# Attention and a gated product on one core: three loads issued by ScalarE, the second weights laid four rows to a partition, and four written orders shifted

## The chip, the cores and the metric

The kernel runs on one core of one Trainium2 chip. The core has five engines that run their own instruction streams: TensorE (PE, with its weight loads shown apart as PEld), VectorE (DVE), ScalarE (ACT), GpSimd (POOL) and SyncE (SP), which here only issues DMAs. The metric is the device time of one execution in microseconds, from the first instruction to the last transfer.

## The reference

Eight batches of eight heads, 576 positions, 64 values a head. Every position attends to those at most 32 away; then every token (a row of 512 = 8 heads x 64) goes through two products with a gelu between.

```python
scores = q @ k.T / sqrt(64)                  # per batch and head, 576 x 576
scores = where(|i - j| <= 32, scores, -1e9)
attn   = softmax(scores);  x = attn @ v      # then 4608 tokens x 512
h      = x @ w_in                            # 512 -> 2048
g      = 0.5 * h * (1 + tanh(sqrt(2/pi) * (h + 0.044715 * h**3)))
out    = g @ w_out                           # 2048 -> 512, fp32
```

All inputs and the output are fp32 in the chip's memory; on the chip the kernel computes in fp16 with fp32 sums.

## The kernel before, in words

**Tiles of tokens.** The 4608 tokens are nine tiles of 512 (t = 0 to 8), which straddle the batches of 576. A stage of the loop over t (line 893) does the first product of tile t, 16 blocks of 128 hidden units ("columns") by four 128-row parts of w_in (`ffn_in`, line 526), each followed by a gelu on ACT (`gelu`), and then the second product. Into the steps of that second product the attention of batch t + 1 is woven. Attention of batch 0 stands ahead of the loop.

**Weights.** w_in (512 x 2048) and w_out (2048 x 512) are read once, in quarters of 1 MB, as fp32 into buffers of a ring of five (`stage`), and cast to fp16 into w_in16 and w_out16, which stay. The SBUF layout of w_out16 is 16 row blocks of 512 columns; row block fc must hold the rows that belong to the hidden units of column block fc of w_in16. Before, both are in natural order: partition p of row block fc is row 128 fc + p (`w_out_v`, line 227), and the casts of w_in (`cast_w`, line 240; lines 835 to 849 and 875) copy 512 columns straight. w_in's casts are shared by POOL, ACT and DVE, w_out's by POOL, ACT and DVE inside tile 0's second product.

**Loads.** Nearly all loads are issued by SP in the order of the program: queries and keys of batch 0 in pairs of heads (`qk`), the keys' tail (positions 512 to 575, `tails_0`), the values' tail (`vs(4)`, line 256), the values of each head (`v_of_pair`), the quarters of w_in, and then w_out's quarters mixed with the queries, keys and values of batch 1 (lines 822 to 861). The query tail of batch 0 (line 852) and the values' tail of batch 1 (in `vs(2, 3, 4)`, line 859) stand among them. "wo3b" below is the second half of the last quarter of w_out (line 860), which holds row blocks 14 and 15.

**Orders written out by hand.** No planner places the work: the program's order is each engine's order. Four tables set it around the change.

- ORDER_0 (line 70) is the order of tile 0's second product, 64 matmuls of 512 columns: steps 0 to 47 take row blocks 0 to 11, each for four token blocks, steps 48 to 55 blocks 12 and 13, steps 56 to 63 blocks 14 and 15.
- PLAN_0 (line 53) names what is put ahead of which step: "s" scores of a group of two heads (4 groups, and -1, the tail), "m" its mask on DVE, "r" the transposes of a pair and their copies, "k" the casts for them, "w" and "u" casts of w_out, "e" casts and "d" copies of the values, "n" the sums of two groups with their logarithms on ACT, "p" the products with the values, "v" both for one group, "x" the division into xT, "c" differences of w_out for later.
- PLAN_1 (line 66) is the same for tile 1 with its 112 matmuls of 256 columns; PLAN serves the later ones.
- MIX (line 62) is the first product of tiles 7 and 8, of which half the columns go by seven block products for two units, A and B, with sums instead of eight (Winograd's form): a number is a plain column, "A3" a block product, "s" a copy of a bank, "c" a sum with one, "g" a gelu, "t" and "u" the sums that the second product needs. In `in_mixed` (line 600) the copies "s" are on ACT for n = 1 and on DVE else.

The second product of tiles 1 to 8 (`ffn_out`, line 700) is also in Winograd's form: seven products of 16 matmuls, whose results DVE reads and adds (lines 730 to 757).

Of the kernel before, what the change touches and what calls it, by code (L numbers as in the profile page):

```python
# [9 lines left out]
FP32 = mybir.dt.float32  # L10
# [26 lines left out]
def cut(b):  # L37
# [12 lines left out]

PLAN_0 = {4: "s0@0", 9: "r1@1", 14: "s1@0", 15: "w1", 16: "m0", 19: "k2", 22: "r2@1", 23: "m1", 25: "s2@0", 27: "t-1@1",
# [3 lines left out]

MIX = ("3 g3 A0 s0A B0 s0B A2 B2 cA00 cB00 A1 s1A A4 B1 s1B gA00 gB00 B4 t0 u0 12 A3 s3A B3 s3B g12 cA11 cB11 13 "
       "A5 B5 gA11 gB11 g13 14 gA10 gB10 A6 B6 cA01 cB01 g14 15 gA01 gB01 t1 t2 g15 t3 u1 u2 u3").split()
UNITS = {"A": 1, "B": 2}

PLAN_1 = {12: "s0@0 s1@1 s2", 16: "m0 m1", 36: "m2", 56: "s-1@0 v0@1 v1", 64: "m-1", 66: "x0", 74: "x1",
          78: "s3@0 v2 v-1@1", 84: "m3", 90: "x2", 93: "x-1", 97: "v3 s4@1", 112: "x3 m4"}
PAIR_1 = {38: slice(0, 4), 50: slice(4, 8)}

ORDER_0 = [(t4, 4 * w + i) for w in range(3) for i in ((0, 2, 3, 1), (0, 2, 1, 3), range(4))[w] for t4 in (0, 1, 3, 2)] + \  # L70
# [8 lines left out]
def kernel(  # L79
# [9 lines left out]
    nc = tc.nc  # L89
    B, H, S, D = q.shape  # L90
# [20 lines left out]
    tailp = ctx.enter_context(tc.tile_pool(name="tailp", bufs=1))  # L111
# [23 lines left out]
    raws, vrs = {}, {}  # L135

    def load_early(b):


        qr = rawp.tile([128, H, 256], FP32, name="qr")  # L140
        kr = rawp.tile([128, H, 256], FP32, name="kr")
        raws[b] = [qr, kr, None]

        def qk(h0, queues=(nc.sync, nc.sync)):
            for src, dst, queue in zip((q, k), (qr, kr), queues):
                queue.dma_start(
                    dst[:, h0:h0 + 2, :],
                    src[b, h0:h0 + 2, 0:512, :].rearrange("h (p j) d -> p h (j d)", j=4))

        def vs(*cs):  # L150
            if len(raws[b]) < 4:
                raws[b].append(stage.tile([128, 4, H, 64], FP32, name="vr", tag="stage"))
                raws[b].append(tailp.tile([64, H, 64], FP32, name="vt", tag="vt"))
            for c in cs:
                if c == 4:
                    nc.sync.dma_start(raws[b][4], v[b, :, 512:S, :].rearrange("h p d -> p h d"))
# [4 lines left out]
        def tails(which="qk"):  # L161
            if raws[b][2] is None:
                raws[b][2] = tailp.tile([128, H, 64], FP32, name="tr", tag="tr")
            tr = raws[b][2]
            if "q" in which:
                nc.sync.dma_start(tr[0:64, :, :], q[b, :, 512:576, :].rearrange("h s d -> s h d"))
# [57 lines left out]
            copy(V[0:64, 3 + c, :, :], V[0:64, c, :, :])  # L224

    w_in_v = moe_w_in.rearrange("(c p) f -> p c f", p=128)
    w_out_v = moe_w_out.rearrange("(c p) f -> p c f", p=128)

    def stage_w():
        return stage.tile([128, 4, 512], FP32, name="wst", tag="stage")  # L230
# [3 lines left out]
        return w  # L234

    def load_w_out(i, w, c0=0, c1=4):
        nc.sync.dma_start(w[:, c0:c1, :], w_out_v[:, 4 * i + c0:4 * i + c1, :])
        return w

    def cast_w(w, dst, on_dve=(0, 1), cs=range(4), on_act=()):  # L240
        for c in cs:
            (nc.scalar.copy if c in on_act else nc.vector.tensor_copy if c in on_dve else nc.gpsimd.tensor_copy)(  # L242
                dst[:, c, :], w[:, c, :])

    qk, tails_0, vs = load_early(0)
    qk(0, (nc.sync, nc.scalar))
# [6 lines left out]
        for h in (2 * g + x for x in hs):  # L253
            nc.sync.dma_start(raws[0][3][:, :, h, :], v[0, h, 0:512, :].rearrange("(c p) d -> p c d", p=128))  # L254

    vs(4)
    for g in range(3):
        v_of_pair(g)
    wi = [stage_w()]
# [340 lines left out]
    def in_mixed(t):  # L600
        if "A" not in mixed:
            mixed["A"] = rawp.tile([128, 3, 512], FP32, name="sa", tag="qr")
            mixed["B"] = rawp.tile([128, 3, 512], FP32, name="sb", tag="kr")

        place = {"00": (0, "b"), "01": (1, "c"), "11": (2, "c")}
        for step in MIX:
            kind, rest = step[0], step[1:]
            if kind in UNITS:
                in_product(kind, int(rest))
            elif kind == "s":  # L610
                n, unit = int(rest[0]), rest[1]
                (nc.scalar.copy if n == 1 else nc.vector.tensor_copy)(
                    mixed[unit][:, (0, 1, None, 2)[n], :], phs[unit, "a"])
            elif kind == "c":
                x, which = place[rest[1:]]
                x = mixed[rest[0]][:, x, :]
                nc.vector.tensor_tensor(x, phs[rest[0], which], x, op=ALU.add)
            elif kind == "g" and rest[0] in UNITS:
                r, c, j = int(rest[1]), int(rest[2]), UNITS[rest[0]]
                src = phs[rest[0], "a"] if rest[1:] == "10" else mixed[rest[0]][:, place[rest[1:]][0], :]  # L620
                nc.scalar.activation(gTs[t][:, 8 * r + 2 * j:8 * r + 2 * j + 2, 256 * c:256 * c + 256],  # L621
                                     src.rearrange("p (h c) -> p h c", h=2), AF.Gelu_apprx_tanh)
            elif kind == "g":
                fc = column(t, int(rest))
                nc.scalar.activation(gTs[t][:, fc, :], phs[fc], AF.Gelu_apprx_tanh)
# [193 lines left out]
    values(0, nc.gpsimd.tensor_copy)  # L819
    values(1, nc.gpsimd.tensor_copy)  # L820

    qk, tails, vs = load_early(1)
    qk(0)
    wo = [load_w_out(0, stage_w())]
    qk(2)
# [6 lines left out]
    spin(2, 512, s0[:, 1, :])  # L832
    values(2, nc.gpsimd.tensor_copy)
    finish(2, s0[:, 0, :])
    nc.gpsimd.tensor_copy(w_in16[:, 0, 0:512], wi[0][:, 0, :])
    nc.scalar.copy(w_in16[:, 1, 0:512], wi[0][:, 1, :])
# [6 lines left out]
    nc.gpsimd.tensor_copy(w_in16[:, 2, 0:512], wi[0][:, 2, :])  # L843
    nc.scalar.copy(w_in16[:, 3, 0:512], wi[0][:, 3, :])
# [10 lines left out]
    vs(0)  # L855
    load_w_out(2, wo[2], 2, 4)
    vs(1)
    wo.append(load_w_out(3, stage_w(), 0, 2))
    vs(2, 3, 4)
    load_w_out(3, wo[3], 2, 4)  # L860
    tails()

# [14 lines left out]
    quarter(2, 0, 1, 2, 3)  # L877
    cast_early(1, 0, split)
# [14 lines left out]
    for t in range(NT):  # L893
# [56 lines left out]
        for i in range(113 if t else 65):  # L950
# [122 lines left out]
```

## Time and profile before

| | us |
|---|---|
| three runs: median (lowest, highest) | 299.79 (298.92, 301.08) |
| the profiled execution | 298.75 |
| its span (first to last instruction) | 297.0 |
| PE busy | 286.2 (96%) |
| DVE busy | 211.0 (71%) |
| ACT busy | 194.8 (66%) |
| POOL busy | 90.3 (30%) |

All times below are microseconds from the start of the span. The profile names instructions by the line of the kernel, the operation, and what is written from what is read. "Busy" counts an instruction from start to end; matmuls overlap, so a row of them costs less than the sum of single ones. The idle time in brackets is that of the engine just before the instruction, with what ended it. A line such as L242 is that of a helper (`cast_w`), which serves w_in and w_out alike.

The stages lie so: attention of batch 0 until about 21, the first product of tile 0 from 21.1 to 34.0, its second product with the attention of batch 1 to 55.7, the stage of tile 1 to 87.4, then stages of some 30.5 each; tile 7 begins near 240, tile 8 near 266, and the last output leaves at 297.

### The profile page before, as it was taken

To read this page: it belongs to the slowest core of one execution; us is meant where nothing else is said; L and a number is where in the kernel's file an instruction comes from. 1 tells how busy PE (TensorE), PEld (TensorE's weight loads), DVE (VectorE), ACT (ScalarE), POOL (GpSimd) and SP (SyncE) were. 2 spreads that over 40 slices of the span, in tenths; PEclk is the share of its full clock that TensorE was granted. 3 is DMA by queue.
4 is the path that set the end of the run, shared out by engine and by line. 5 is a ranking of instruction groups with operands and counts; after the bars stand their busy time and mean duration, and the time that the engine had idled before them with its cause. 6 is when DMAs were issued, how large, how long until landed. Compare 5 with 4: busy or idle time off the path is not lost.

```text
span 297.0 us, 7284 instructions
## 1 busy us (share of the span) xinstructions
PE 286.2 (96%) x2949; PEld 184.4 (62%) x2949; DVE 211.0 (71%) x468; ACT 194.8 (66%) x313; POOL 90.3 (30%) x141
## 2 busy tenths in 40 slices
PE   7889999999999999999999999999999999999994
PEld 2534444546774588458844884488547867787683
DVE  4573577997986676868686879576966767865772
ACT  5865766778577876678657965695669556706700
POOL 3426425202419631506080606060800050015000
PEclk9999999999999999999999999999999999999999
DMA  7999999999999995899996997999694040004013
GB/s 217 236 306 383 370 291 267 265 181 201 293 214 195 276 224 106 139 155 227 161 205 113 246 150 176 125 226 170 100 192 25 0 113 32 2 11 134 0 36 108
DMA packets 116616, 51.02 MB, mean 172 GB/s; under 512 B 98391, under 2 KB 110167, under 8 KB 116582
## 3 DMA queue, kind: packets, MB, share of 16 engines
q1 hardware_dynamic: 91684, 38.67, 60.9%
q0 software_dynamic: 23776, 10.83, 23.3%
q10 hardware_dynamic: 1122, 1.06, 1.1%
q8 instruction: 23, 0.38, 0.6%
q14 instruction: 11, 0.09, 0.1%
HBM read 36.70 MB, written 9.44 MB: 155 GB/s over the span
## 4 chain that ended last, share of the span: by engine, by line
PE 83%; DVE 5%; DMA 3%; ACT 3%; SPq 3%; issue 1%; DVEq 0%
PE mm L719 31%; PE ph L545 18%; PE mm L545 17%; PE ps_s L436 3%; PE ps_d L463 2%; SPq L254 2%; PE pu L597 2%; PE ps_o L473 2%; ACT gT L621 2%; PE mm L691 2%; DMA vr<-in_v_dram 2%; PE py L691 2%; DVE s L662 2%; DMA kr<-in_k_dram 1%; PE ps_od L463 1%; PE ps_od L473 1%
## 5 line engine op out<-in xcount | busy, mean ns | idle before, releaser
L545 PEld LDWEIGHTS <-w_in 128*128 128x128 f16 x512 | 49.7, 98 | 56.2 <-DVE w_in L242 0.4
L545 PE MATMUL ph<-xT,w_in 128*128 128x512 f16 x256 | 64.1, 379 | 0.0
L545 PE MATMUL mm<-xT,w_in 128*128 128x512 f16 x256 | 64.1, 379 | 0.0
L681 POOL DMA_DIRECT2D out_dram<-y x55 | 32.3, 596 | 84.0 <-DVE y L748 75.6
L553 ACT ACTIVATE gT<-mm 128x512 f16<-128x512 f32 x60 | 35.6, 598 | 33.1 <-PE mm L545 32.5
L719 PEld LDWEIGHTS <-s 128*128 128x128 f16 x512 | 49.2, 98 | 7.6 <-issue 0.9
L719 PE MATMUL mm<-t,s 128*128 128x256 f16 x376 | 45.2, 273 | 0.6 <-DVE y L732 0.2
L662 DVE TENSOR_TENSOR s<-gT 128x512 f16<-128x512 f16 x64 | 27.1, 423 | 21.3 <-ACT gT L553 20.3
L719 PEld LDWEIGHTS <-gT 128*128 128x128 f16 x384 | 36.2, 98 | 6.8 <-issue 0.5
L553 ACT ACTIVATE gT<-ph 128x512 f16<-128x512 f32 x58 | 32.2, 600 | 10.7 <-PE ph L545 10.7
L449 ACT ACTIVATE pe<-ps_s 128x960 f16<-128x960 f32 (+1 forms) x31 | 29.6, 975 | 12.6 <-PE ps_s L436 12.4
L719 PE MATMUL mm<-w_out,gT 128*128 128x256 f16 x256 | 32.6, 273 | 0.0
L104 ACT ACT_TABLE_LOAD x18 | 23.1, 1283 | 2.2 <-issue 1.9
L498 ACT ACTIVATE lt<-ps_d 128x480 f32<-128x480 f32 (+2 forms) x28 | 15.6, 556 | 12.1 <-PE ps_d L463 8.1
L499 ACT ACTIVATE lt<-lt 128x480 f32<-128x480 f32 (+3 forms) x36 | 21.1, 585 | 1.1
L458 DVE TENSOR_TENSOR pe<-pe,band 128x960 f16<-128x960 f16 x28 | 18.5, 680 | 1.0 <-ACT pe L449 1.0
L473 PEld LDWEIGHTS <-V 128*64 128x64 f16 x520 | 13.8, 112 | 7.2 <-DVE V L218 2.0
L719 PE MATMUL mm<-t,gT 128*128 128x256 f16 x128 | 16.2, 273 | 0.0
L662 DVE TENSOR_TENSOR s<-s,gT 128x512 f16<-128x512 f16 x32 | 14.2, 444 | 1.1
L208 POOL DMA_DIRECT2D V<-in_v_dram x16 | 14.3, 909 | 1.4 <-PE mm L719 0.7
L719 PE MATMUL mm<-w_out,s 128*128 128x256 f16 x120 | 14.6, 273 | 0.0
L508 DVE TENSOR_TENSOR xT<-ps_o,lt 128x480 f16<-128x480 f32 (+5 forms) x26 | 13.4, 535 | 1.1 <-PE ps_o L473 1.1
(146 smaller groups left out, 388.2 us busy)
## 6 DMA issues: line engine op xcount, KB each, us to landing
kr<-in_k_dram SPq DMA_DIRECT2D x31, 256.0 KB, 12.0
qr<-in_q_dram SPq DMA_DIRECT2D x6, 1024.0 KB, 6.7
wst<-in_moe_w_in_dram SPq DMA_DIRECT2D x7, 512.0 KB, 8.5
wst<-in_moe_w_out_dram SPq DMA_DIRECT2D x2, 1024.0 KB, 11.0
wst<-in_moe_w_out_dram SPq DMA_DIRECT2D x4, 512.0 KB
qr<-in_v_dram SPq DMA_DIRECT2D x8, 256.0 KB, 5.8
V<-in_v_dram POOLq DMA_DIRECT2D x16, 128.0 KB, 9.1
qr<-in_q_dram SPq DMA_DIRECT2D x7, 256.0 KB, 6.9
```

The lines of the kernel that those rows point to most:

```text
L104: nc.scalar.add_instruction(mybir.InstLoadActFuncSet(name=nc.get_next_instruction_name(), act_func_set_id=which, ins=[], outs=[]))
L208: nc.gpsimd.dma_start(V[:, c, :, :], v[b, :, 128 * c:128 * c + 128, :].rearrange("h p d -> p h d"))
L449: nc.scalar.activation(pe, ps[:, :, 0:w], AF.Exp, scale=SCALE)
L458: nc.vector.tensor_tensor(pe, pe, m.rearrange("k (o j) p -> k o j p", o=1).broadcast_to(list(pe.shape)), op=ALU.mult)
L473: nc.tensor.matmul(o[64 * h:64 * h + 64, cols].rearrange("d (j p) -> d j p", j=4)[:, :, p0 - q0:p1 - q0], Vs[b % 2][:, slot, 2 * pr + h, : ...
L498: nc.scalar.activation(lt[:, 0:n], d[:, 0:n], AF.Ln)
L499: nc.scalar.activation(lt[:, 0:n], lt[:, 0:n], AF.Exp, scale=-1.0)
L545: nc.tensor.matmul(ph, w_in16[:, dc, fc * 128:fc * 128 + 128], xT[:, dc, t * 512 % RING:t * 512 % RING + 512], start=(dc == 0), stop=(dc = ...
L553: nc.scalar.activation(gTs[t][:, fc, :], phs[fc], AF.Gelu_apprx_tanh)
L662: nc.vector.tensor_tensor(dst, x, y, op=op)
L681: eng.dma_start(out_v[b, j, q0 + p:q0 + p + e, cols], yo[m:m + e, cols])
L719: nc.tensor.matmul(pys["apart"][:, 0:256] if apart else py[:, blk, :], lhsT, wino[w][:, f, :], start=(new and i % (8 if one else 16) == 0) ...
```

## The change

Five things, all in one diff.

1. Three loads go from SP's queue to ACT's: the values' tail of batch 0 (after the bias copies instead of ahead of the values), the query tail of batch 0 (after the gelus of the third four columns instead of among w_out's quarters), and the values' tail of batch 1 (ahead of step 30 of tile 0's second product instead of ahead of wo3b).
2. w_out is read as `(i p c) f -> i p c f` with c = 4: partition p of quarter i holds the four adjacent rows 512 i + 4 p to 4 p + 3, 8 KB in one piece (4 KB for half a quarter), where before four rows lay 128 apart, 2 KB each.
3. The casts of w_in (`cast_in`) put column 512 i + 4 p + j at place p of block 4 i + j, so that column blocks and row blocks hold the same hidden units. Their source is read at a step of four fp32 values; the target is written in a row as before. The engines of the casts are the same.
4. PLAN_0, PLAN_1 and MIX are rewritten, and in MIX's copies "s3B" goes from DVE to ACT.
5. The band copies on DVE (`band_out`) go behind the first key cast of batch 1.

PE has the same 2949 matmuls, in another order in tile 0's second product and in tiles 7 and 8.

```diff
-PLAN_0 = {4: "s0@0", 9: "r1@1", 14: "s1@0", 15: "w1", 16: "m0", 19: "k2", 22: "r2@1", 23: "m1", 25: "s2@0", 27: "t-1@1",
-          29: "w2", 33: "s-1@1 n0@0", 35: "e0", 36: "m2", 37: "k3", 38: "w5", 39: "m-1", 40: "r3@1", 43: "e1",
-          46: "s3@0 v-1@1 d0", 47: "w3 e2", 48: "d1 m3", 51: "n2@0", 52: "e3 d2 d3 x-1",
-          55: "u3 p0@0 p2@1 x0 x1", 56: "e4 x2 x3", 60: "c1"}
+PLAN_0 = {4: "s0@0", 9: "r1@1", 14: "s1@0", 15: "w1", 16: "m0", 19: "k2", 22: "r2@1", 23: "m1", 28: "s2@0 w2",
+          29: "t-1@1", 34: "s-1@1 n0@0", 35: "e0", 36: "m2", 37: "k3", 38: "w5", 39: "m-1", 41: "r3@1", 43: "e1",
+          47: "s3@0 v-1@1 d0 w3 e2", 48: "m3 d1", 52: "e3 d2 d3 x-1", 53: "n2@0",
+          55: "u3", 57: "p0@0 p2@1 x0 x1", 58: "e4 x2 x3", 60: "c1"}
...
-MIX = ("3 g3 A0 s0A B0 s0B A2 B2 cA00 cB00 A1 s1A A4 B1 s1B gA00 gB00 B4 t0 u0 12 A3 s3A B3 s3B g12 cA11 cB11 13 "
-       "A5 B5 gA11 gB11 g13 14 gA10 gB10 A6 B6 cA01 cB01 g14 15 gA01 gB01 t1 t2 g15 t3 u1 u2 u3").split()
+MIX = ("3 g3 A0 s0A B0 s0B 12 g12 A2 B2 cA00 cB00 A1 s1A gA00 A4 B1 s1B gB00 B4 t0 u0 13 g13 A3 s3A B3 s3B 14 g14 "
+       "cA11 cB11 A5 gA10 B5 gB10 gA11 gB11 A6 B6 cA01 cB01 15 gA01 gB01 t1 t2 g15 t3 u1 u2 u3").split()
...
-PLAN_1 = {12: "s0@0 s1@1 s2", 16: "m0 m1", 36: "m2", 56: "s-1@0 v0@1 v1", 64: "m-1", 66: "x0", 74: "x1",
-          78: "s3@0 v2 v-1@1", 84: "m3", 90: "x2", 93: "x-1", 97: "v3 s4@1", 112: "x3 m4"}
+PLAN_1 = {12: "s0@0 s1@1 s2", 16: "m0 m1", 36: "m2", 56: "s-1@0 v0@1 v1", 62: "m-1 x0", 64: "x1",
+          78: "s3@0 v2 v-1@1", 79: "m3", 88: "x2", 91: "x-1", 97: "v3 s4@1", 112: "x3 m4"}
...
-    w_out_v = moe_w_out.rearrange("(c p) f -> p c f", p=128)
+    w_out_v = moe_w_out.rearrange("(i p c) f -> i p c f", p=128, c=4)
...
-        nc.sync.dma_start(w[:, c0:c1, :], w_out_v[:, 4 * i + c0:4 * i + c1, :])
+        nc.sync.dma_start(w[:, c0:c1, :], w_out_v[i, :, c0:c1, :])
...
+    def cast_in(copy, i, c):
+        copy(w_in16[:, c, 512 * i:512 * i + 512].rearrange("k (j p) -> k j p", j=4),
+             wi[i][:, c, :].rearrange("k (p j) -> k j p", j=4))
...
-    vs(4)
...
+    vs(4, queue=nc.scalar)
     nc.vector.memset(ones, 1.0)
...
-                (nc.scalar.copy if n == 1 else nc.vector.tensor_copy)(
+                (nc.scalar.copy if n == 1 or rest == "3B" else nc.vector.tensor_copy)(
...
-    cast_w(wi[1], w_in16[:, :, 512:1024], (0, 2))
-    cast_w(wi[2], w_in16[:, :, 1024:1536], (0, 2))
+    for i in (1, 2):
+        for c in range(4):
+            cast_in(nc.vector.tensor_copy if c in (0, 2) else nc.gpsimd.tensor_copy, i, c)
...
-    tails_0("q")
...
-    vs(2, 3, 4)
+    vs_1(2, 3)
     load_w_out(3, wo[3], 2, 4)
...
-    cast_w(wi[3], w_in16[:, :, 1536:2048], (0, 2))
-    band_out()
+    for c in range(4):
+        cast_in(nc.vector.tensor_copy if c in (0, 2) else nc.gpsimd.tensor_copy, 3, c)
     quarter(2, 0, 1, 2, 3)
+    tails_0("q", nc.scalar)
     cast_early(1, 0, split)
+    band_out()
...
+            if t == 0 and i == 30:
+                vs_1(4, queue=nc.scalar)
```

More of the change, by code (lines that the diff above doesn't have):

```diff
@@ L148, in qk, with vs @@
                     src[b, h0:h0 + 2, 0:512, :].rearrange("h (p j) d -> p h (j d)", j=4))
-        def vs(*cs):
+        def vs(*cs, queue=nc.sync):
             if len(raws[b]) < 4:
@@ L155, in vs @@
                 if c == 4:
-                    nc.sync.dma_start(raws[b][4], v[b, :, 512:S, :].rearrange("h p d -> p h d"))
+                    queue.dma_start(raws[b][4], v[b, :, 512:S, :].rearrange("h p d -> p h d"))
                 else:
@@ L159, in vs, with tails @@
                                       v[b, :, 128 * c:128 * c + 128, :].rearrange("h p d -> p h d"))
-        def tails(which="qk"):
+        def tails(which="qk", queue=nc.sync):
             if raws[b][2] is None:
@@ L165, in tails @@
             if "q" in which:
-                nc.sync.dma_start(tr[0:64, :, :], q[b, :, 512:576, :].rearrange("h s d -> s h d"))
+                queue.dma_start(tr[0:64, :, :], q[b, :, 512:576, :].rearrange("h s d -> s h d"))
             if "k" in which:
@@ L254, in v_of_pair @@
             nc.sync.dma_start(raws[0][3][:, :, h, :], v[0, h, 0:512, :].rearrange("(c p) d -> p c d", p=128))
-    vs(4)
+    raws[0].append(stage.tile([128, 4, H, 64], FP32, name="vr", tag="stage"))
+    raws[0].append(tailp.tile([64, H, 64], FP32, name="vt", tag="vt"))
     for g in range(3):
@@ L820 @@
     values(1, nc.gpsimd.tensor_copy)
-    qk, tails, vs = load_early(1)
+    qk, tails, vs_1 = load_early(1)
     qk(0)
@@ L834 @@
     finish(2, s0[:, 0, :])
-    nc.gpsimd.tensor_copy(w_in16[:, 0, 0:512], wi[0][:, 0, :])
-    nc.scalar.copy(w_in16[:, 1, 0:512], wi[0][:, 1, :])
+    cast_in(nc.gpsimd.tensor_copy, 0, 0)
+    cast_in(nc.scalar.copy, 0, 1)
     values(3, nc.vector.tensor_copy)
@@ L842 @@
     load_table(gelu_set)
-    nc.gpsimd.tensor_copy(w_in16[:, 2, 0:512], wi[0][:, 2, :])
-    nc.scalar.copy(w_in16[:, 3, 0:512], wi[0][:, 3, :])
+    cast_in(nc.gpsimd.tensor_copy, 0, 2)
+    cast_in(nc.scalar.copy, 0, 3)
     for dc in range(2, 4):
@@ L847 @@
             ffn_in(0, n, dc, dc + 1)
-    cast_w(wi[1], w_in16[:, :, 512:1024], (0, 2))
-    cast_w(wi[2], w_in16[:, :, 1024:1536], (0, 2))
+    for i in (1, 2):
+        for c in range(4):
+            cast_in(nc.vector.tensor_copy if c in (0, 2) else nc.gpsimd.tensor_copy, i, c)
     wo.append(load_w_out(1, stage_w()))
     qk(4)
-    tails_0("q")
     wo.append(load_w_out(2, stage_w(), 0, 2))
     qk(6)
-    vs(0)
+    vs_1(0)
     load_w_out(2, wo[2], 2, 4)
-    vs(1)
+    vs_1(1)
     wo.append(load_w_out(3, stage_w(), 0, 2))
-    vs(2, 3, 4)
+    vs_1(2, 3)
     load_w_out(3, wo[3], 2, 4)
@@ L874 @@
     quarter(1, 0, 1, 2, 3)
-    cast_w(wi[3], w_in16[:, :, 1536:2048], (0, 2))
+    for c in range(4):
+        cast_in(nc.vector.tensor_copy if c in (0, 2) else nc.gpsimd.tensor_copy, 3, c)
+    quarter(2, 0, 1, 2, 3)
+    tails_0("q", nc.scalar)
+    cast_early(1, 0, split)
     band_out()
-    quarter(2, 0, 1, 2, 3)
-    cast_early(1, 0, split)
     quarter(3, 0, 1)
```

## The prediction

> **What bounds the kernel now.** I read the page's chain first, then PE by stage, then the timeline around each place where PE stood still, then the records of DMA packets.
>
> ```profile
> PE 83%; DVE 5%; DMA 3%; ACT 3%; SPq 3%; issue 1%; DVEq 0%
> ```
>
> TensorE (PE) carries 83% of the chain, and its clock was granted in full in all 40 slices. A change that removes no matmul, as this one, can only win PE's pauses. Busy time by stage says how many there are (columns: stretch, length, busy time of PE, PEld, DVE, ACT, POOL with instruction counts, clock, DMA share, GB/s):
>
> ```profile
> 20.90:34.04 13.14, 13.14 (x79) 5.89 (x75) 6.17 (x16) 7.69 (x15) 6.34 (x8) 1.00 1.06 380
> 34.04:55.71 21.67, 20.77 (x248) 10.23 (x248) 15.34 (x33) 16.33 (x29) 9.18 (x14) 1.00 1.09 291
> 55.71:87.35 31.64, 31.29 (x356) 20.76 (x355) 27.82 (x60) 23.52 (x39) 5.56 (x9) 1.00 1.07 226
> 87.35:118.00 30.65, 30.65 (x337) 20.28 (x335) 21.02 (x43) 23.02 (x36) 15.04 (x23) 1.00 1.14 203
> ```
>
> The first product of tile 0 (row 1) and the stages from tile 2 on (row 4) have no pause. The second product of tile 0 (row 2) has 0.90 us, the stage of tile 1 (row 3) 0.35. A lone 512-column matmul shows 379 ns and a row of them 216 ns each, so each pause shows some 0.16 us too short. The places:
>
> ```profile
> 42.07 0.40 PE L436 MATMUL ps_s<-QT,KT 64*64 64x96 f16 x16 [0.49 <-ACT KT L358]
> 51.19 0.39 PE L463 MATMUL ps_od<-pe,ones 128*64 128x480 f16 x2 [0.23 <-DVE pe L458]
> 52.70 1.12 PE L473 MATMUL ps_od<-pe,V 128*64 128x96 f16 x56
> 52.90 0.61 POOL L242 CAST w_out<-wst 128x512 f16<-128x512 f32 x1 [1.29 <-DMA wst<-in_moe_w_out_dram]
> 53.98 0.59 PE L691 MATMUL mm<-w_out,gT 128*128 128x512 f16 x2
> 81.88 0.42 PE L473 MATMUL ps_o<-pe,V 128*64 128x96 f16 x14 [0.32 <-DVE xT L508]
> 254.90 2.19 PE L719 MATMUL mm<-t,s 128*128 128x256 f16 x16
> ```
>
> Row 1: the scores of group 2 wait for the transposed keys. Row 2: the sums of group 3 wait for its mask. Row 3 waits for ACT's logarithms (PE was free at 52.38). Rows 4 and 5 are a near miss: the cast of w_out's row block 14 ends at 53.51, and PE uses it at 53.98. Last row: 16 matmuls of 109 ns and the modelled tail of 0.17 should take 1.91.
>
> **The change, part by part.**
>
> *Order of tile 0's second product (PLAN_0).* s2 goes from step 25 to 28: six matmuls (1.30 us) instead of three cover the turn of the keys, which takes 1.08 (40.95 to 42.03), so the 0.49 goes. n2 goes from 51 to 53 and the mask m3 ahead of chunk copy d1 (0.92 with its waits on DVE): 0.39 goes (50.80 to 51.19). p0/p2 go from 55 to 57: the 0.32 before 52.70 goes. But p0/p2 (1.05 of PE work) no longer stand ahead of step 56, the first use of row block 14. PE gets there at 53.98 - 1.05 - 1.20 = 51.73 instead of 53.98, and the block is cast at 53.51 as before, unless its load lands earlier. So **the next bound is the last half of w_out**. From its cast there are 8 matmuls (1.73), p (1.05) and a handover of 0.05 to tile 1: tile 1 starts at 53.51 + 2.83 = 56.34 minus what the load gains, against 55.71: +0.63 minus the gain, and at best -1.20 when the load gains 1.8.
>
> *Second weights, four rows to a partition, and three loads by ACT.* The records of packets by size show the DMA engines as one line that never empties from 19 to 48 us; w_out's last packets end at 52.08. w_out goes in 2 KB packets of 84 ns on one engine; the trace's 4 KB packets later take 160. For the 3.5 MB ahead of that cast: 1,792 x 84 / 16 = 9.4 us against 896 x 160 / 16 = 9.0, so 0.45 us saved; bounds 0 (same bytes) and 1.2 (nothing in the trace shows 8 KB packets of data; I take a tenth of 9.4 and the 0.3 us by which w_out's last issue trails the line at 49.8). [...] So load and order together give +0.63 - 0.5 = **+0.1 us** for tile 0 (-0.6 to +0.8).
>
> [...]
>
> ACT pays by issue time. Its two issues at the start took 0.50 and 0.49; SP's up to 2.35 under load; I take 0.6 and keep 2.3. The first stands after the bias copies, where ACT is idle 1.04 before the keys' copy (5.82); the second in an idle 0.87 before the copy at 32.36, whose reader comes at 35.01 and behind which the activations wait for PE until 33.66; the third beside an idle 0.94 before the tail's exponential (44.94). At 2.3 each, the third would hold that exponential, n0's logarithms and r3's buffer by 1.4, all before step 56, where PE waits anyway. Cost 0, at worst 0.4.
>
> *Casts in the new column order.* Each w_in cast reads fp32 at a step of four.
>
> ```profile
> L242 POOL CAST w_in<-wst 128x512 f16<-128x512 f32 x6 | 5.2, 869 | 5.3 <-DMA wst<-in_moe_w_in_dram 5.3
> L242 DVE CAST w_in<-wst 128x512 f16<-128x512 f32 x6 | 2.6, 427 | 5.3 <-DMA wst<-in_moe_w_in_dram 5.3
> L358 DVE COPY KT<-pt 128x512 f16<-128x512 f16 x5 | 3.4, 679 | 0.0
> L357 DVE COPY QT<-pt 128x512 f16<-128x512 f16 x8 | 3.4, 422 | 5.1 <-PE pt L352 3.6 <-PE pt L350 1.5
> ```
>
> No row shows such a read from SBUF. The nearest is on DVE, from PSUM: KT's copy reads with a step and takes 679, QT's of one size without takes 422. So DVE's cast costs 0.43 to 0.69; I take 0.6. ACT's KT copy (586) is no slower than its casts (603 to 618): 0. POOL has no such row: 0.87 from below (less if DVE no longer slows it: alone it took 0.614), 0.87 x 1.61 = 1.40 by DVE's ratio, 4 x 0.61 = 2.4 if the bytes stepped over were all read. I take 1.2, next to DVE's ratio. The loads land 1.3 to 1.5 us apart (casts start at 22.50, 23.80, 25.16, 26.47, 28.00, 29.36), so 1.2 keeps pace; the query cast behind them (30.21, 0.70) then ends at 31.3, and PE transposes it at 31.60. Only the first DVE cast (22.47) has PE waiting, +0.2, and that is swallowed by the wait at step 56. Band copies now behind the key cast (1.73 us): masks read the band at 38.38. Cost 0.
>
> [...]
>
> *PLAN_1.* x1 moves from 74 to 64, m-1 and x0 ahead of DVE's read of product 3. DVE then does m-1 (0.55, from 78.85), x0 (0.71), that read (0.65) and x1 (0.71, its logarithm being there at 80.45), and ends at 81.47 instead of 81.82: of the 0.32 + 0.16 at 81.88, **-0.35** goes (0 to -0.48). The mask m3 five steps earlier delays a product read by 0.3, which nobody waits for within 16 matmuls.
>
> *MIX, tiles 7 and 8.* PE runs the mixed stage without a gap (14 x 0.434 + 4 x 0.864 from 243.17 to 252.71); then the second product waits for sums, which wait for ACT:
>
> ```profile
> 250.15 0.63 ACT L621 ACTIVATE gT<-sa 128x512 f16<-128x512 f32 x1 [1.60 <-DVE sa L617]
> 254.23 0.62 ACT L625 ACTIVATE gT<-mm 128x512 f16<-128x512 f32 x1
> ```
>
> From 250.15 nine activations run end to end, 0.48 to 0.60 apart. The new order moves columns 12 to 14 ahead and s3B from DVE to ACT, into the idle 1.60. Then the closed run is eight long and starts when PE ends column 14: from A0 at 243.17 ten products (4.34) and three columns (2.59), 250.1, and 0.2 to ACT: 250.3. So it starts 0.15 later and is one of 0.50 shorter: the sums come 0.35 earlier, twice, **-0.7**. The pauses there are 0.27 + 0.28 in tile 7 and 0.17 more in tile 8, so between 0 and -1.27. Column 12 now follows B0 and shares a bank with column 3, read until 244.14, PE being there at 244.04: 0.1, before a pause, so free.
>
> **The sum** against the profiled execution (298.75: span 297.0 and 1.75 around it): +0.1 - 0.35 - 0.7 = -0.95, 297.8. The median of the three runs, 299.79, is 1.04 higher, the lowest is 298.92; the same sum gives 298.8 from the median. I forecast 298.2, between the two. No change can be told within 1% here.
>
> **Rivals.**
> - *The w_out half lands no earlier* (20%): vt's packets come in ahead of it and the larger packets save nothing. Tile 0 +0.8, the rest -1.05 or less: 298.5 to 299.3. For it: same engines, same bytes. Against: fewer packets.
> - *The load gains over a microsecond* (12%): the order's full win, tile 0 -0.6 to -1.2, with -0.48 and -1.2 elsewhere: 296 to 297.
> - *Slower: POOL's strided cast* (13%). Six run in a row from 22.50, then the query cast: 22.5 + 6d + 0.7 against PE's 31.60. PE waits from d = 1.4 us. Above, it loses 6 x (d - 1.4), while w_out lands behind that cover, so the rest wins its full -1.2 - 1.05 = -2.25. It decides from 1.8, where the two are even; at 2.4 it is +3.75: 302.5. Against it: 1.40 by DVE's ratio.
>
> The forecast itself (297.2 to 298.8) has 55%. The range 296.3 to 300.8 leaves out the far ends of the second and third rivals. Faster by over 1% needs most pauses won, 0.07; slower by over 1% needs POOL above 2.3 us, 0.08.
>
> **What would show it.** POOL and DVE casts of w_in (1.2, 0.6); the cast of block 14 with a DMA wait ahead of it and PE idle before step 56 (about 1 us, from 51.7); no pause at s2, n2, p0; x1 near 80.7; the last activation of column 15 0.35 earlier against A0. A PE pause before the transposes at 31.6, or w_out packets slower than 84 ns for 2 KB, would make it wrong.

## The result, and the profile after

| | before | after |
|---|---|---|
| median of six runs each (lowest, highest) | 299.83 (298.92, 305.7) | 302.21 (301.92, 302.89) |
| ratio of times, 95% interval | | 1.0068 (1.0042 to 1.0094) |
| the profiled execution | 298.75 | 302.25 |
| its span | 297.0 | 300.5 |

The change costs 2.4 us by the medians, 0.7% by the ratio. The forecast was 298.2 with 296.3 to 300.8, and its chances left 0.85 for a time within 1%: the measured time lies above the range, although inside 1%. The two profiled executions differ by 3.5, more than the medians, since the one of before was shorter than any of its timed runs. I account for these 3.5 first.

| us from the start of the span | before | after | this part adds |
|---|---|---|---|
| first product of tile 0 starts | 18.45 | 21.69 | +3.24 |
| its second product starts | 34.04 | 38.24 | +0.96 |
| tile 1 starts | 55.71 | 59.43 | -0.48 |
| tile 2 starts | 87.35 | 90.65 | -0.42 |
| tile 8 starts | 266.22 | 269.48 | -0.04 |
| last matmul | 292.39 | 295.55 | -0.10 |
| end of the span | 297.02 | 300.53 | +0.35 |

So the whole loss, 4.2 us, stands ahead of tile 0's second product, where I had booked nothing; 1.04 comes back behind it, and 0.35 goes after the last matmul. The page of after, its clock in 40 slices and its chain by engine:

```profile
PEclk9599999999999999999999999999999999999998
...
PE 89%; ACT 3%; DVE 3%; DMA 2%; SPq 1%; issue 1%; ACTq 0%; DVEq 0%
```

The second slice (7.5 to 15.0 us) has half the clock, which before had in full. The stages of after, in the same columns as those of before (stretch, length, busy PE, PEld, DVE, ACT, POOL, clock, DMA share, GB/s):

```profile
21.69:38.24 16.55, 15.15 (x94) 6.95 (x89) 13.36 (x22) 10.79 (x18) 10.22 (x11) 1.00 1.05 385
38.24:59.43 21.19, 20.66 (x248) 10.45 (x246) 13.99 (x30) 16.49 (x29) 7.22 (x10) 1.00 1.16 257
59.43:90.65 31.22, 31.15 (x355) 20.74 (x354) 27.83 (x60) 23.55 (x39) 5.22 (x8) 1.00 0.85 180
90.65:121.29 30.64, 30.64 (x336) 20.26 (x334) 21.77 (x43) 22.97 (x36) 14.13 (x22) 1.00 1.17 208
```

The first product holds PE busy for 15.15 of 16.55 us, where before it had no pause from 20.90 on; the two stages behind it lost pauses, as forecast. First the lines of before that these places are compared with; then the timeline of after, with several engines in order of time. A line with SPq or ACTq is the issue of a load by that engine; the line numbers differ between the two kernels.

```profile
3.16 1.62 ACT L294 COPY xT<-xT 64x160 f16<-64x160 f16 x6
5.82 0.59 ACT L358 COPY KT<-pt 128x512 f16<-128x512 f16 x1 [1.04 <-PE pt L352]
7.28 0.39 PE L436 MATMUL ps_s<-QT,KT 64*64 64x96 f16 x16
20.08 0.29 DVE L217 COPY V<-V 64x512 f16<-64x512 f16 x1
20.40 0.28 DVE L218 COPY V<-V 64x384 f16<-64x384 f16 x1
251.00 0.60 PE L597 MATMUL pu<-xT,wcA 128*128 128x256 f16 x4
```

```profile
3.99 0.79 ACT L299 COPY xT<-xT 64x160 f16<-64x160 f16 x3
8.64 0.75 ACTq L156 DMA_DIRECT2D vt<-in_v_dram  x1
9.44 0.58 ACT L364 COPY KT<-pt 128x512 f16<-128x512 f16 x1 [4.65 <-DMA kr<-in_k_dram]
10.07 0.64 PE L442 MATMUL ps_s<-QT,KT 64*64 64x96 f16 x16 [2.50 <-ACT KT L364]
...
22.68 1.17 POOL L246 CAST w_in<-wst 128x512 f16<-128x512 f32 x1 [0.21 <-DMA wst<-in_moe_w_in_dram]
22.93 1.08 DVE L217 COPY V<-V 64x512 f16<-64x512 f16 x1
23.14 0.60 PE L551 MATMUL ph<-xT,w_in 128*128 128x512 f16 x2 [0.42 <-ACT w_in L246]
24.03 1.09 POOL L246 CAST w_in<-wst 128x512 f16<-128x512 f32 x1 [0.18 <-DMA wst<-in_moe_w_in_dram]
24.04 1.23 DVE L218 COPY V<-V 64x384 f16<-64x384 f16 x1
25.32 0.40 PE L479 MATMUL ps_o<-pe,V 128*64 128x64 f16 x14 [0.97 <-DVE V L218]
...
42.41 0.40 PE L442 MATMUL ps_s<-QT,KT 64*64 64x96 f16 x16
54.71 0.60 PE L469 MATMUL ps_od<-pe,ones 128*64 128x480 f16 x4
56.43 1.21 PE L479 MATMUL ps_od<-pe,V 128*64 128x96 f16 x56 [0.16 <-ACT lt L1000]
57.92 0.38 PE L697 MATMUL mm<-w_out,gT 128*128 128x512 f16 x1 [0.28 <-ACT w_out L242]
85.17 0.40 PE L479 MATMUL ps_o<-pe,V 128*64 128x96 f16 x14
...
254.67 0.60 PE L603 MATMUL pu<-xT,wcA 128*128 128x256 f16 x4
256.47 0.63 ACT L627 ACTIVATE gT<-sa 128x512 f16<-128x512 f32 x1
257.60 0.58 ACT L631 ACTIVATE gT<-mm 128x512 f16<-128x512 f32 x1
258.23 2.12 PE L725 MATMUL mm<-t,s 128*128 128x256 f16 x16
```

The first four lines of after carry the result. ACT's load of the values' tail stands in its program after the bias copies, which end near 4.8. It is issued at 8.64 only, just after a load of keys has landed (its last part at 8.62 in the trace); the keys' copy stands behind it and comes at 9.44, where before it came at 5.82. PE waits 2.50 for it, until 10.07, and from within that wait the clock is granted at half, from 8.6 to 15.4. Then, in lines 5 to 10, DVE's value copies take 1.08 and 1.23 beside POOL's casts (0.29 and 0.28 before), and PE waits 0.97 for them. The pauses at s2 (42.41), n2 (54.71) and in tile 1 (85.17) are gone or too short to be listed; 0.16 of that at p0 (56.43) is left, and a matmul at 57.92 waits 0.28 for ACT's cast of w_out.

The casts of w_in by engine (count, busy time, mean ns, idle time before):

```profile
L246 POOL CAST w_in<-wst 128x512 f16<-128x512 f32 x8 | 9.4, 1175 | 4.0 <-DMA wst<-in_moe_w_in_dram 3.9
L246 DVE CAST w_in<-wst 128x512 f16<-128x512 f32 x6 | 5.6, 994 | 0.0
L246 ACT CAST w_in<-wst 128x512 f16<-128x512 f32 x2 | 2.2, 1104 | 0.0
```

All three engines need about 1.0 to 1.2 us a cast here. POOL is as predicted (1.2) in this profile. ACT, costed at nothing, went from 0.60 (603 and 618 ns before) to 1.10.

### The profile page after: what moved, and what is told of

The parts are those of the page before. It is cut to its first block, busy times and chain, and to the rows that moved or that the text cites. A ratio compares the mean times of both kernels' runs of the same rounds, so it can differ in the third digit from the quotient of the medians.

```text
span 300.5 us, 7282 instructions
## 1 busy us (share of the span) xinstructions
PE 288.2 (96%) x2949; PEld 185.7 (62%) x2949; DVE 215.5 (72%) x466; ACT 197.4 (66%) x315; POOL 92.2 (31%) x141
## 3 DMA queue, kind: packets, MB, share of 16 engines
HBM read 36.70 MB, written 9.44 MB: 154 GB/s over the span
## 4 chain that ended last, share of the span: by engine, by line
PE 89%; ACT 3%; DVE 3%; DMA 2%; SPq 1%; issue 1%; ACTq 0%; DVEq 0%
PE mm L725 32%; PE ph L551 18%; PE mm L551 18%; PE ps_s L442 4%; PE pu L603 3%; PE ps_d L469 2%; PE ps_o L479 2%; PE py L697 2%; DMA kr<-in_k_dram 2%; PE mm L697 2%; PE mm L603 1%; PE ps_od L469 1%; DVE V L218 1%; PE pt L356 1%; ACT gT L559 1%
## 5 line engine op out<-in xcount | busy, mean ns | idle before, releaser
L442 PE MATMUL ps_s<-QT,KT 64*64 64x128 f16 (+3 forms) x576 | 13.9, 221 | 2.8 <-ACT KT L364 2.5
L442 PEld LDWEIGHTS <-KT 64*64 64x64 f16 x576 | 10.4, 110 | 9.2 <-issue 4.2
```

Source lines behind the costliest of these rows:

```text
L442: nc.tensor.matmul(sides[h][64 * half:64 * half + 64, 4 * n * r:4 * n * r + 4 * n].rearrange("k (j p) -> k j p", j=4)[:, :, p0 - q0:p1 - q ...
```

## The experiments

Two theories stood after this reading. **W**: a load waits on the engine that issues it for an earlier load to land, and holds the work behind it; here the keys' copy. **C**: the stepped casts cost it all. Ratios are to runs of the kernel before on the same chip, with 95% intervals; "second product" is its start in the profiled execution (before 34.04, after 38.24).

| kernel | ratio (interval) | median | second product | tile 1 |
|---|---|---|---|---|
| vt_by_sp | 0.9995 (0.9957, 1.0033) | 300.42 | 34.19 | 60.09 |
| plain_casts | 0.9992 (0.9966, 1.0018) | 299.96 | 35.45 | 57.04 |
| both_undone | 0.9987 (0.9960, 1.0014) | 300.32 | 33.42 | 56.55 |
| vt_alone | 1.0038 (1.0015, 1.0061) | 301.52 | 37.30 | 58.82 |
| casts_alone | 0.9981 (0.9959, 1.0003) | 299.89 | 34.44 | 56.36 |
| keep_clock | 1.0093 (1.0063, 1.0122) | 303.28 | 37.52 | 58.72 |
| plans_alone (4 runs) | 1.0110 (1.0066, 1.0154) | 303.96 | 37.28 | 62.30 |
| plans_again (12 runs, same kernel) | 1.0015 (0.9984, 1.0047) | 300.55 | 34.05 | 58.93 |
| plan1_mix | 0.9987 (0.9959, 1.0015) | 299.76 | 35.16 | 56.81 |
| vt_behind | 1.0400 (1.0348, 1.0453) | 314.33 | 51.45 | 72.69 |
| plans_p55 | 0.9967 (0.9936, 0.9999) | 300.47 | 35.85 | 57.44 |
| plans_act | 0.9995 (0.9961, 1.0030) | 301.47 | 36.56 | 58.50 |
| combo | 0.9968 (0.9932, 1.0004) | 300.05 | 33.89 | 56.08 |
| combo_again (same kernel) | 0.9975 (0.9944, 1.0006) | 299.56 | 34.34 | 55.93 |
| vt_first | 0.9957 (0.9926, 0.9988) | 299.08 | 34.30 | 58.63 |
| v3_by_act | 1.0073 (1.0043, 1.0102) | 302.57 | 37.99 | 59.53 |
| after_p55 | 1.0076 (1.0041, 1.0111) | 303.03 | 37.83 | 59.12 |
| first_p55 | 0.9952 (0.9926, 0.9977) | 298.83 | 34.10 | 56.86 |

The median of before on these chips was 300.3 to 300.8. Places come from one execution and spread by more than a microsecond between executions of one kernel: plans_alone and plans_again are the same program, and the profiled executions of vt_by_sp (303.42) and vt_first (303.20) were the longest of ten. So places show mechanisms, and the ratios decide on time.

### Undoing the load, the casts, and both; the load alone

```diff
 vt_by_sp:    -    vs(4, queue=nc.scalar)      +    vs(4)            (SP, ahead of v_of_pair)
 plain_casts: -w_out_v "(i p c) f -> i p c f"  +"(c p) f -> p c f";  cast_in without its rearranges
 both_undone: both
 vt_alone:    before, with only vs(4) moved to ACT behind the bias copies
```

> The changed kernel with the values' tail of batch 0 issued by SyncE again, ahead of the values, all else as changed. Theory W (the load on ScalarE waits for an earlier load and holds the keys' copy behind it): ScalarE's idle 4.65 us before that copy is gone, the clock stays full, and the second product of tile 0 starts at 35.0 to 35.5 instead of 38.24 (3.2 us back, the casts' 1 us stays); time 299.0 to 299.5. Theory C (the stepped casts cost all of it): the start stays above 37.5, time near 302.

> The changed kernel with w_out in natural rows and the casts of w_in straight, the three loads still on ScalarE. Theory W: ScalarE's idle of 4.65 us and the half clock stay, only the casts' share comes back, some 1.0 to 1.4 us; time 300.8 to 301.3. Theory C: the time falls to 298.5.

> The changed kernel with both undone: values' tail of batch 0 by SyncE, natural rows, straight casts. What is left is the three tables, the query tail of batch 0 and the values' tail of batch 1 by ScalarE. By both theories the second product of tile 0 starts at 34.0 again; the tables' gains as measured in the changed kernel's later stages (0.5 in tile 0's second product, 0.4 in tile 1, 0.1 in tile 7) stay: 298.0 to 298.8, which is 0.3 to 0.6% below the kernel before. If the gains come only because the first product was late, it is the time before, 299.8.

> The kernel before with one edit: the values' tail of batch 0 issued by ScalarE after the bias copies. Theory W: ScalarE idle 4 to 5 us before the keys' copy, half clock for some 7 us, the second product of tile 0 later by 3 us, time 302.3 to 303. Theory C: no difference, 299.8.

Either undoing gives the whole loss back, and both together no more than one. The load alone costs 0.38%: W's mechanism holds, at 1.2 us, not at all of the loss. In vt_alone ACT idles 5.19 before the keys' copy, its load goes out at 9.18 when the load of keys has landed at 9.16, and the clock is at half from 10.1 to 16.9. The sizes missed in all four: vt_by_sp took longer than W said (300.42 for 299.0 to 299.5), plain_casts and vt_alone less (299.96 for 300.8 to 301.3, 301.52 for 302.3 to 303), and both_undone, with 300.32, showed none of the gain (298.0 to 298.8) that both theories gave it. C is not the whole either, but the casts take part: with the load as changed, plain casts save 0.76%. The timeline of plain_casts at the place where after had its slow value copies:

```profile
21.87 0.29 DVE L217 COPY V<-V 64x512 f16<-64x512 f16 x1
22.19 0.28 DVE L218 COPY V<-V 64x384 f16<-64x384 f16 x1
22.30 0.61 POOL L246 CAST w_in<-wst 128x512 f16<-128x512 f32 x1 [0.74 <-DMA wst<-in_moe_w_in_dram]
```

The copies are late too, by 1.8 against before (22.93 in after), but take 0.29 and 0.28 beside POOL's short casts. In the profiles the first product takes 15.59 before, 15.82 with stepped casts on time (casts_alone), 14.82 late with plain casts (vt_alone), and 16.55 late with stepped casts (after). So the two parts meet: lateness alone does not lengthen it, the step alone by 0.2, both by 1 to 1.7.

### The casts alone, the clock, the value copies

> The kernel before with the second weights' rows and the stepped casts alone (all loads, orders and plans as before). Theory C2: a stepped cast costs about 1.1 us on every engine, slows VectorE's value copies beside it, and has TensorE wait in the first product; tile 0's second product then starts at 35.0 to 35.5 (before 34.04), and with p0 and p2 still ahead of step 56 at most 0.3 us of that is given back: 301.0 to 301.6 where before shows 300.3, 1.002 to 1.005 of it. Rival, by the prediction's step (VectorE 0.6, ScalarE free, GpSimd 1.2, all covered): second product at 34.2 to 34.4, 300.0 to 300.5.

Its edit is the second weights' rows and `cast_in` put into the kernel before. It came out at 0.9981, at or below the rival's figure: on time, the slower casts cost no time that these runs show, as the prediction's step had it, and C2 falls.

```diff
 keep_clock, in after:
+    spin(10)
     score(0, 0, 0)
```

> The changed kernel with ten more idle matmuls ahead of group 0's scores, into the 2.50 us for which TensorE waits for the keys' copy. Theory W: the half clock from 8.6 to 15.4 us came of that pause and cost about 1 us of the 4.2 by which the second product was late; with it gone the clock stays full, the second product starts at 36.8 to 37.4 (38.24 without), and 0.6 to 1.2 us come off: 301.0 to 301.6 where the changed kernel shows 302.2. Rival: the copy and the casts set that stretch and the clock costs nothing: 38.0 to 38.4 and 302.0 to 302.5.

The clock stayed full (0.996 over the span) and the second product came at 37.52, 0.7 earlier than in after; but the time, 1.0093, is no better (the profiled 301.6 was the shortest of its eight runs). The half clock is a mark of the wait, and no run shows a price of its own for it; Theory W's 0.6 to 1.2 us fell.

```diff
 v3_by_act, in after:
-        pair_v(0, nc.vector.tensor_copy, hs)
+        pair_v(0, nc.scalar.copy if g == 3 else nc.vector.tensor_copy, hs)
```

> The changed kernel with the two value copies of group 3 by ScalarE instead of VectorE, which took 1.08 and 1.23 us beside GpSimd's stepped casts (0.29 and 0.28 where no such cast ran). Theory P (GpSimd's long casts hold VectorE's copies, and TensorE waits 0.97 us for the second): ScalarE's copies take 0.3 to 0.6 each, TensorE's wait there is under 0.3, the second product starts at 37.2 to 37.7 (38.24), 301.2 to 301.7 where the changed kernel shows 302.2. Rival (another wait takes its place, for ScalarE's casts behind the copies): 38.0 to 38.6, 302.0 to 302.6.

```profile
22.69 0.62 ACT L217 COPY V<-V 64x512 f16<-64x512 f16 x1
23.34 0.51 ACT L218 COPY V<-V 64x384 f16<-64x384 f16 x1
...
26.31 0.61 PE L551 MATMUL ph<-xT,w_in 128*128 128x512 f16 x2 [1.05 <-ACT w_in L246]
```

The copies take 0.62 and 0.51 on ACT and PE's wait for them is gone, but ACT's cast, behind them, is now 1.05 late. The rival holds: 1.0073. With everything 3 us late, taking one wait away shows the next, here on ACT.

### Where the load may stand

```diff
 vt_behind, in after:
-    vs(4, queue=nc.scalar)          (behind the bias copies)
     score(0, 0, 0)
+    vs(4, queue=nc.scalar)
```

> The changed kernel with ScalarE's first load (the value tails) issued behind its exponential of group 0 instead of ahead of the keys' copy; all three loads stay on ScalarE. Theory W (it is the place ahead of the keys' copy that costs, since the load waits for an earlier one to land and holds the copy): ScalarE's keys' copy back at 5.5 to 6.5 us, no half clock before 20 us, tile 0's second product at 34.0 to 35.2, and the time where the kernel with that load by SyncE stood: 0.997 to 1.001 of before. Rival (loads by ScalarE cost whatever their place): 1.004 to 1.007, second product at 37 or later.

```profile
12.10 0.73 ACTq L156 DMA_DIRECT2D vt<-in_v_dram  x1
12.88 0.60 ACT L503 ACTIVATE lt<-ps_d 128x512 f32<-128x512 f32 x1 [3.69 <-PE pt L357]
...
19.90 0.60 POOL L331 CAST V<-vt 64x512 f16<-64x512 f32 x1 [8.98 <-DMA vt<-in_v_dram]
21.09 9.89 DVE L217 COPY V<-V 64x512 f16<-64x512 f16 x1 [8.06 <-POOL V L818]
22.11 8.17 POOL L246 CAST w_in<-wst 128x512 f16<-128x512 f32 x8
```

A large miss that taught most. The keys' copy did come back to 5.99, but the wait went with the load: now it held the logarithm of group 0 by 3.69. The listing of ACT's built program says why:

```
after     vs(4): DMACopy vt<-in_v_dram  waits DMAHW6   (a load of keys, eight loads before it)
vt_behind vs(4): DMACopy vt<-in_v_dram  waits DMAHW3   (a load of values, eight loads before it)
vt_first  vs(4): DMACopy vt<-in_v_dram  no wait
```

Eight completion semaphores (DMAHW0 to 7) go round among the loads of SP and ACT. In the trace of before the first eight of these loads wait for none; of the next 47, 40 wait on the semaphore that they report on themselves, which the load eight before was the last to use, and seven, four of them w_out's, on one that no load reports on. All of these are SP's, where only other loads stand behind them. The times agree: the last part of that earlier load lands at 8.62 in after and at 12.08 in vt_behind, and ACT's load starts at 8.64 and 12.10. In vt_behind the tail then landed only at 19.9; POOL, whose casts stand in order, waited 8.98 for it, and then ran its casts of values, w_in and a query without a gap from 20.45 to 30.8, beside which one value copy on DVE (0.29 elsewhere) lasted 9.89.

```diff
 vt_first, in after:
     qk(4)
+    vs(4, queue=nc.scalar)          (the eighth load as written)
     qk(6)
 ...
-    vs(4, queue=nc.scalar)
```

> The changed kernel with ScalarE's first load (the value tails) moved to be the eighth load of all, so that no load stands eight ahead of it; all three loads stay on ScalarE. Theory W2 (a load waits, on the engine that issues it, for the load eight before it in the program to land, and holds that engine's work): ScalarE's keys' copy at 5.8 to 6.6 us, no half clock before 20 us, tile 0's second product at 34.0 to 35.5, 0.997 to 1.002 of before. Rival (ScalarE's issues as such, or the tails' packets ahead of the keys of the later chunks, cost as much): second product at 36.5 or later, 1.004 to 1.007.

```profile
1.87 0.76 ACTq L156 DMA_DIRECT2D vt<-in_v_dram  x1
2.66 1.28 ACT L104 ACT_TABLE_LOAD   x1 [2.66 <-issue]
...
6.00 0.59 ACT L362 COPY KT<-pt 128x512 f16<-128x512 f16 x1 [0.41 <-PE pt L356]
...
53.62 0.61 POOL L242 CAST w_out<-wst 128x512 f16<-128x512 f32 x1 [1.55 <-DMA wst<-in_moe_w_out_dram]
54.28 0.52 PE L695 MATMUL mm<-w_out,gT 128*128 128x512 f16 x1 [2.14 <-POOL w_out L242]
```

The same three loads by ACT, the same casts, the same orders, and 0.9957 of before: 1.1% under the changed kernel, and better than W2's 0.997 to 1.002. This settles W in its second form (W2): not ACT's queue and not the issue's length (0.76 here, 0.75 in after), but the landing that the load waits for. The last two lines show the near miss that the prediction had named, PE before step 56. This profiled execution took 303.20 against a median of 299.08, so 2.14 is an upper end.

### The order of tile 0's second product

> The kernel before with PLAN_0 and PLAN_1 of the changed kernel alone. Theory A (the prediction's step on row block 14): the first product is on time (second product at 34.0), and TensorE stands before step 56 for 1 to 2 us, waiting for GpSimd's cast of that block, which waits for its load; tile 1 starts at 56.3 to 56.7 (before 55.71), its stage takes 31.2 (before 31.64): 300.3 to 300.9 where before shows 300.3. Rival (the block is there in time): tile 1 at 54.5 to 55.0, 298.7 to 299.2.

> The same kernel as plans_alone, in more runs. Theory A: TensorE waits 1 to 2.5 us before step 56 in the profile, and it stays slower than before: 1.004 to 1.012. Rival (the first four runs were unlucky): 0.998 to 1.003.

> The kernel before with PLAN_0 and PLAN_1 of the changed kernel, but n2 at step 51 and p0 and p2 at step 55 as before, so that 1.05 us of TensorE's work stands ahead of step 56 again. Theory A (the order without that cover lost 3.6 us because TensorE waits there over 2 us for a late load, and then gets half the clock for 3.4 to 6.8 us): the wait before step 56 is under 0.5 us, no half clock there, 0.996 to 1.000 of before. Rival (it was not the cover, but something else in the order, or the loads of those runs): 1.006 to 1.012.

```diff
 plans_p55, in plans_alone:
-  53: "n2@0", 55: "u3", 57: "p0@0 p2@1 x0 x1", 58: "e4 x2 x3"
+  51: "n2@0", 55: "u3 p0@0 p2@1 x0 x1", 56: "e4 x2 x3"
```

plans_alone is the kernel before with PLAN_0 and PLAN_1 alone. PE does wait before step 56, in both of its profiles (2.14 and 2.04 us), and the clock is then at half for 3.4 us. The first product was on time in plans_again only; in plans_alone the second product starts 3.2 late, which Theory A did not have. From plans_again:

```profile
54.03 0.61 POOL L242 CAST w_out<-wst 128x512 f16<-128x512 f32 x1 [2.27 <-DMA wst<-in_moe_w_out_dram]
54.70 0.58 PE L691 MATMUL mm<-w_out,gT 128*128 128x512 f16 x1 [2.04 <-POOL w_out L242]
```

With p0 and p2 ahead of it again the wait is gone (plans_p55, and also combo and first_p55 below), and the ratio 0.9967. But the 1.1% of the first four runs shrank to 0.15% in twelve, inside the rival's 0.998 to 1.003, so the price of the missing cover lies between nothing and 1%, and how late the load is differs from execution to execution: the last half of w_out landed at 52.08 in the profile of before and at 55.96 in that of plans_alone.

> The changed kernel with n2 at 51 and p0 and p2 at 55 as before. Since its first product is 4 us late, the second weights are there in time and no wait stands before step 56: I expect no difference, 1.005 to 1.009 of before. Rival (step 56 has a hidden share): 1.000 to 1.004.

after_p55 has the same three entries in the changed kernel: 1.0076, no difference, as expected. With the first product some 4 us late the load was there in both profiles.

> The kernel before with PLAN_0 and PLAN_1 of the changed kernel as they are, and the two later loads (query tail, value tails of the second image) by ScalarE; value tails of the first image by SyncE, rows and casts as before. Theory L (these two loads out of SyncE's queue let the last half of the second weights start earlier, which pays for the cover taken away): the last half lands 0.8 to 1.5 us earlier than in the kernel with the plans alone, against the loads ahead of it, and the time is 0.998 to 1.003 of before. Rival (its order among the loads decides nothing): 1.007 to 1.013 as with the plans alone.

plans_act (query tail and second values' tail to ACT) against plans_again is 0.9995 against 1.0015, inside both intervals: whether these two loads gain anything in time stays open. The earlier landing that Theory L asked for is not seen: w_out's last packets end at 53.83, where plans_again has 52.95 and plans_alone 55.96. In its profile PE waits 0.27 before step 56.

### PLAN_1 and MIX, and the versions put together

> The kernel before with PLAN_1 and MIX of the changed kernel alone. Theory M (as the changed kernel's stages show): tile 1's stage 31.2 instead of 31.64, tiles 7 and 8 each 0.1 shorter: 299.6 to 299.9 where before shows 300.3, 0.9975 to 0.999 of it. Rival, the prediction's sizes (0.35 for tile 1 and 0.35 for each mixed tile): 299.1 to 299.4, 0.996 to 0.997.

0.9987, with an interval (0.9959 to 1.0015) that holds both figures; the stages decide for theory M. Tile 1's is 31.17 (before 31.64), and tile 7's 26.40 (26.51), the latter to 0.01 in every profile with the new MIX.

> The changed kernel with the value tails of the first image loaded by SyncE as before, and n2 at 51 and p0 and p2 at 55 as before: the two places that the runs so far blame are taken back, the rest stays. If the parts add (rows and casts 0.998, PLAN_1 and MIX 0.9987): 0.995 to 0.998 of before, 299.0 to 299.7 where before shows 300.3. Rival (they do not add, since a late load sets tile 1's start): 0.998 to 1.001.

> The same kernel as combo (value tails of the first image by SyncE, n2 at 51, p0 and p2 at 55, the rest as changed), in more runs. 0.995 to 0.999 of before, with an upper end of the interval below 1; rival: 1.000 within its interval.

combo is vt_by_sp with the three entries of plans_p55. Two measurements, 0.9968 and 0.9975, each with an interval that just reaches 1, so that a gain over before isn't shown. In one of its profiles PE also lost 1.42 in a later tile, waiting for a transposed load of keys, a spread that shows in several kernels:

```profile
225.37 0.62 PE L440 MATMUL ps_s<-QT,KT 64*64 64x96 f16 x32 [1.42 <-DMA KT<-k]
```

> The changed kernel with the value tails as the eighth load of all and with n2 at 51 and p0 and p2 at 55 as before: every place blamed is mended, all else as changed. Theory A: no wait over 0.5 us before step 56, and a little under the kernel with the tails first alone: 0.993 to 0.997 of before. Rival (the order there is worth nothing on most runs): 0.995 to 0.999.

first_p55 is vt_first with those three entries: 0.9952 (0.9926 to 0.9977), 298.83 against 300.30. It beats the kernels before and after, and so does vt_first; the two can't be told apart.

## Why the prediction was wrong, step by step

- **The step that failed: "ACT pays by issue time ... Cost 0, at worst 0.4."** I priced an issue by its own duration (0.5 to 2.3) and looked for idle time on ACT to hold it. The duration was near enough, 0.75 for 0.6. But the load first waited for one eight before it to land (8.62 in after), and that wait, put at nothing, held ACT: the keys' copy went from 5.82 to 9.44, the first product from 18.45 to 21.69. vt_first, in which this load waits for none, turns 1.0068 into 0.9957. Applied to the median of before that the forecast used, 299.79, this is 298.5, inside the forecast's own 297.2 to 298.8. That is partly luck: the terms below did not hold one by one.
- **Casts, "ACT ... 0":** 1.10 for 0.60, wrong. POOL's mean is 1.18 in after (1.2 predicted) with DVE's at 0.99 (0.6 predicted); in vt_first, on time, it is 1.43 with DVE's at 0.72. Between these two profiles the one got longer and the other shorter, which I had not priced. That the casts are covered was right in time while the first product is on time (casts_alone 0.9981) and wrong 3 us later, where DVE's value copies run beside them. The slower rival, POOL's cast from 1.4 us on, is not what cost 4 us in after, but it did come true in small where the rest is on time. In vt_first the six casts in a row take 1.5 each, the query cast behind them ends late, and PE waits 0.47 before the transposes (0.33 in first_p55), which the prediction had named as a sign of being wrong:

```profile
22.09 4.48 POOL L246 CAST w_in<-wst 128x512 f16<-128x512 f32 x3 [2.46 <-DMA wst<-in_moe_w_in_dram]
32.12 0.40 PE L354 MATMUL pt<-idn,q 128*128 128x128 f16 x4 [0.47 <-POOL q L326]
```

- **PLAN_0:** the three pauses went as worked out but for 0.16 at p0, and the wait before step 56 took their place, about 1 us predicted from 51.7; in the profiles of kernels with the new PLAN_0 whole and the first product on time it is 1.48 (both_undone), 2.04 (plans_again), 2.14 (vt_first) and 2.62 (vt_by_sp), the last two in long executions. The half clock in three of the four was not foreseen. In the changed kernel the wait is not there, because all before it is late: its second product is 0.48 shorter.
- **w_out's larger packets and the load's gain of 0.5:** no run shows a gain. w_out's last packets landed at 51.3 to 53.2 in the profiles of the kernels with the new rows and a first product on time (combo, first_p55, vt_first, casts_alone), at 52.08 in that of before, and executions spread by more. Nor did an earlier issue bring an earlier landing each time: the issue of the last half ended at 49.06 before and at 46.84 and 47.20 in combo and combo_again, which are one program, and the last packets at 52.08, 51.32 and 52.70. The two later loads took ACT 0.63 and 0.60 to issue in after, where SP had taken 1.57 and 2.28.
- **PLAN_1, -0.35:** right in after (-0.42) and plan1_mix (-0.47), and in most other profiles with it. In both_undone (31.62) and plans_p55 (31.61) nothing is left of it: PE waits in another place of the stage, for a copy of the values on DVE.
- **MIX, -0.35 twice:** mis-sized. I let the closed run of eight activations start at PE's end of column 14 and go through without a gap. It starts 7.30 after A0 (7.13 worked out), but its last three (256.47 to 257.60) wait for product 6 and its sums on DVE, which come no earlier: product 6 starts at 254.67, 8.14 after A0 (7.83 before), with the same PE work ahead of it as before and pauses of 0.15 at column 12 (0.1 worked out) and 0.17 just before it. The last activation of the run is 11.07 after A0, where it was 11.06. What is left is -0.11 in tile 7 and -0.10 in tile 8, from PE's shorter pauses; and the profiles with the new MIX end 4.81 to 5.04 after the start of their last matmul (v3_by_act 4.67), those with the old one 4.54 to 4.71. So no run shows a gain by MIX.
- **The range** was too narrow at the top because no rival was a wait in front of the first product: my only case beyond 300.8 was POOL's cast, which stands inside the first product, one stage behind the true place.

## What to carry to other kernels

Where a load is moved to a computing engine, ask which earlier transfer it waits for there, and what stands behind it on that engine: here it waited for none as the eighth load (vt_first, 0.9957), and later it held ACT until an earlier one had landed (ACT idle 4.65 in after, 3.69 in vt_behind). A cost covered when all is on time need not be covered when the stage is late (the stepped casts: 0.9981 of before when alone, 0.76% behind the late load), so price two parts of a change together where one delays the other. Before a late stage is given an order without slack, look at how much the landing of its loads differs between executions (w_out's last half: 52.08 in before, 55.96 in plans_alone).

## What the runs showed of the hardware

- Reading fp32 at a step of four values cost ACT 1.10 us a cast of 128 x 512 (mean of after) instead of 0.60, and POOL 1.07 (mean of vt_behind, where DVE's one copy of 9.89 ran beside all eight) instead of 0.61: some 1.8 times on both.
- A value copy on DVE of 0.29 us lasted 9.89 in vt_behind while POOL ran twelve casts one behind the other; it started at 21.09, during the second, and ended at 30.98, when the last of them had ended at 30.83. In after, copies of 0.29 and 0.28 took 1.08 and 1.23 and ended 0.16 and 0.15 behind casts of POOL. What holds the copies is not shown.
- In these profiles every wait of PE of 2.0 us or more (2.04 in plans_again to 2.92 in vt_alone) came with half the clock, for 3.4 us (plans_again, vt_first) or 6.8 (after, vt_alone), and for 23.9 in vt_behind, where PE waited three times. Of the shorter ones two did (1.48 in plans_p55, mean clock 0.989; 1.72 in plan1_mix, 0.994) and others did not (1.48 in both_undone, mean clock 0.999; 1.88 in vt_first).
- What lengthens the end by some 0.3 us in the profiles with the new MIX stays open. VectorE's last drain stands 4.46 (plan1_mix) to 4.69 (combo_again) behind the start of the last matmul there, 4.05 to 4.23 in those with the old one; but in v3_by_act, which has the new MIX and two copies fewer on DVE, it stands at 4.16.
